# The first unit's rest rows kept in DRAM and multiplied in the last unit, paired with that unit's own

## The chip, the cores and the metric

One core of one Trainium2 chip runs the whole kernel. The metric is the device time of one execution in microseconds; a kernel's time is the median of its runs. In what follows PE is the engine of the matmuls (PEld its weight loads), DVE, ACT and POOL are the vector, scalar and GpSimd engines, and SP is the engine from whose queue nearly all DMAs are issued.

## What is computed

Attention with normalized queries and keys, then a feed-forward block with a squared ReLU:

```
q, k, v: (8, 12, 448, 64)                       # batch, heads, rows, head size
q_n = q / rms(q) * g_q;  k_n = k / rms(k) * g_k
attn = softmax(q_n @ k_n.T / 8) @ v             # for each batch and head
x    = attn put as (8 * 448, 768)               # batch and row, heads side by side
out  = relu(x @ w_in)**2 @ w_out                # w_in (768, 2048), w_out (2048, 768)
```

The weights arrive as 64-bit floats. The kernel loads their words and makes float32 of them itself.

## The kernel before

**Units.** The feed-forward block is done in four units of two batches each (u = 0 to 3, `ffn`). A unit goes through four blocks of the hidden dimension. Each block has a first part (x @ w_in, giving the `hid` tiles) and a second part (hid @ w_out, added into the `acc` tiles). Unit 0's first part is `first_products`: 14 products of COST_IN = 18 in the planner's currency. Later units use `deep_products`. The second part is `second_products`: seven products replace eight (Strassen's scheme in Winograd's form), P1 to P7, over a pair of row tiles, one of each batch of the unit. Each product is two matmuls in the source and four matmul instructions in the trace, because a float32 matmul is issued as two. A product has a cost of COST_OUT = 10.

**Rests.** A batch has 448 rows: three tiles of 128 (NT = 3) and a rest of 64. The two rests of a unit make one tile of 128 rows. Seven products need two such tiles, so a unit's own rests alone can't use them. In units 0 and 3, `multiply_rest` (L1187) multiplies them in the plain way: eight matmuls, 16 instructions, in each block. The rests of units 1 and 2 (`KEPT`) are stored to DRAM block by block (`keep_rests`, L1198), brought back in unit 3 (`bring_rests`, L1214), and multiplied there as one extra pair of tiles by P1 to P7 (tile number NT; its sums are made on POOL by `add_rests`, L1225).

**What a product waits for.** P1 uses a part of `hid` as it stands. P5, P6 and P3 use sums that POOL makes of the four quarters of `hid` (`hidden_sum`, L1173); P7 uses a quarter that POOL changes in place. P5, P6, P7 and P4 also use sums of the output weights (T1 to T4, made at L1539). Three PSUM banks take turns (`roles`); a product may reuse a bank when DVE (L1370) or ACT has taken its contents to an `acc`. In unit 3 the first tile of a block has the order FIRST_OF_BLOCK, in which the two halves of the rests stand where POOL's sums are awaited. In unit 0 the rests come first, before the first P1.

**What is woven into unit 0.** While unit 0 runs, 24 *visits* of attention work for unit 1's batches are put between its products: each gives PE some 8 to 20 instructions (attend L545, score L455) and ACT the exponentials (L463). `run(place(u, x))` lets the products go on until the cost spent reaches a point, then the visit is emitted. Half a visit earlier, tasks are queued that turn the next keys and queries (L367 on DVE, scaled by L377 on ACT). Also in unit 0, the weights of the next blocks are converted in 64 pieces. The call for a piece (`convert`) splits its words on ACT (L1430, L1431, L1433) and joins those of the piece before on DVE (L1444, then L1463 one step later, which gives the buffer back); there are three word buffers, loaded by L1411 (w_in) and L1416 (w_out). The list `late` says at which cost each call is due: before, one every 31.4, evenly. The sums of a finished weight tile are made one at each later step (L1539), and the forms of w_out and of w_in are stored to DRAM for the later units (L1569, L1489, L1517). At the start of block 3's second part the first pieces for unit 1 are loaded back (L902).

**Order.** An engine executes its instructions in the order in which they were emitted. ACT in particular has the copies out of PSUM (L1017), the split of words, the scaling of queries and the exponentials in one row.

Of the kernel before, what the change touches and what calls it, by code (L numbers as in the profile page):

```python
# [225 lines left out]
def program(ctx, tc, rows, v, g, wide, ones, moe_w_in, moe_w_out, out, shift):  # L226
# [711 lines left out]
    FIRST_OF_BLOCK = ["P1", "rest0", "P5", "P4", "P6", "P2", "rest1", "P3", "P7"]  # L938
# [9 lines left out]
    COST_SECOND = (NT * 7 + 4) * COST_OUT  # L948
    COST = NF // 2 * 7 * COST_IN + NBLK * COST_SECOND
    COST_SHORT = NT * 7 * COST_OUT  # L950
    LATER = NBLK * (7 * 11 * COST_DEEP + COST_SHORT)
    KEPT = range(1, B // 2 - 1)
    assert len(KEPT) == 2
# [11 lines left out]
    def ffn(u):  # L965

        accs = []
        for blk in range(NBLK):
# [8 lines left out]
            if u == B // 2 - 1:  # L977
                bring_rests(blk)
                add_rests()
# [195 lines left out]
    PARTS = [(0, 0), (1, 0), (0, 1), (1, 1)]  # L1175
    PARTS_BY_ROW = [(0, 0), (0, 1), (1, 0), (1, 1)]

    def out_of(u, blk):
        return [u * NF // 2 + 2 * blk + t for t in range(2)]

    def multiply_rest(u, blk, hid, places, some, acc=None, halves=range(2)):

        w_sb = [out_sb[n] for n in out_of(u, blk)]
        for half in halves:
            ps = places[half][:, 0:HALF]
            for a, t in some:
                nc.tensor.matmul(  # L1187
                    ps, lhsT=hid[a].rearrange("p t e s -> p t (e s)")[:, t, ds(NT * P, P)],
                    rhs=w_sb[t][:, 2 * a + half, :],
                    start=(a, t) == PARTS[0], stop=(a, t) == PARTS[-1],  # L1190
                )
            if acc is not None:
                add_to(acc[:, ts(half, HALF)], ps, blk == 0)
# [9 lines left out]
    def bring_rests(blk):  # L1203

        if not extra:
            for name in ("11", "12", "S3", "22", "S1", "S2", "S4"):
                some = att.tile([P, S], F32, name="wT", tag="wT", bufs=8)
                extra[name] = some[:, 0 : 2 * P].rearrange("p (t n) -> p t n", t=2)
            extra["accs"] = [
                room.rearrange("p x g h d -> p (x g h d)")[:, 0:DM] for room in rows.rooms  # L1210
            ]
        for u, names in zip(KEPT, (("11", "12"), ("S3", "22"))):
            for a, name in enumerate(names):
                nc.sync.dma_start(extra[name], kept[u][blk, :, a])  # L1214

    def add_rests():

        a11, a12, a21, a22, s1, s2, s4 = [
            extra[name] for name in ("11", "12", "S3", "22", "S1", "S2", "S4")
# [7 lines left out]
    def second_products(u, blk, hid, sums_, accs):  # L1227

        split, final = u in KEPT, u == B // 2 - 1
        if blk == 0:  # L1230
            accs.extend(new_acc() for _ in range(2 * NT if split else 2 * NT + 1))
# [10 lines left out]
        if u:  # L1242
            turn_roles(1, 2, 0)
        else:
            make_sums(0, 1, 2, 3)
            for some in (PARTS[:3], PARTS[3:]):
                multiply_rest(u, blk, hid, roles, some, accs[-1] if (1, 1) in some else None)
                yield len(some) * COST_OUT
            turn_roles(2, 1, 0)

        def store_rows(tt, e, columns=slice(None)):
            if tt is None or tt == NT:
                n = u if tt is None else KEPT[e]
                parts = [(2 * n, P * NT, REST), (2 * n + 1, 0, REST)]
            else:
                parts = [(2 * u + e, REST * e + P * tt, P)]
            store(accs[-1] if tt is None else accs_of(tt)[e], parts, columns)

        def accs_of(tt):
            return extra["accs"] if tt == NT else accs[2 * tt : 2 * tt + 2]  # L1260

        to_store = deque([] if split else [(None, 0)])
# [3 lines left out]
        def product(tt, name, ps, engine):  # L1266
# [5 lines left out]
            for t in range(2):  # L1272
                nc.tensor.matmul(  # L1273
                    ps, lhsT=extra[left][:, t] if tt == NT else lefts[left][:, t, ts(tt, P)],
# [663 lines left out]
```

## Time and profile before

| what | value |
|---|---|
| median of 3 runs | 1381.96 us (1381.06 to 1382.34) |
| the profiled execution: its time / its span | 1381.76 us / 1379.6 us |
| PE busy | 1358.1 us (98% of the span) |
| DVE, POOL, ACT busy | 807.7, 789.8, 608.0 us |
| unit 0 in the span | 129.1 to 487.0 us |
| unit 3 in the span | 1091.8 to 1374.2 us, then the last stores |
| rests, L1187 | 128 matmul instructions, 64 in each of units 0 and 3 |
| products of the second part, L1273 | 1456 matmul instructions, 112 of them on kept rests |

The page gives busy times, the chain of work that ended last, and groups of instructions by line. A busy time of PE counts each matmul from issue to a modelled end, and matmuls overlap; what a matmul costs on the way is read from the chain, where consecutive ones lie end to end. "Idle before, releaser" says what the engine waited for.

### The profile page before, as it was taken

How to read it: one execution, taken by the hardware profiler on the slowest of the kernel's cores; microseconds unless marked ns; L12 is line 12 of the kernel's file. 1: busy time of each engine (PE TensorE's matmuls, PEld its weight loads, DVE VectorE, ACT ScalarE, POOL GpSimd, SP SyncE). 2: the span in 40 equal slices, each digit the busy share in tenths (PEclk: the TensorE clock that was granted, in tenths of full speed). 3: DMA queues.
4: the chain of work that ended last, by engine and by line, in shares of the span. 5: the costliest groups of instructions: out<-in, count | busy, mean ns of one | idle time of the engine just before them, and what ended most of it. 6: DMA issues, size and time to landing. Idle time of an engine off the chain costs nothing.

```text
span 1379.6 us, 19591 instructions
## 1 busy us (share of the span) xinstructions
PE 1358.1 (98%) x6320; PEld 847.1 (61%) x6320; DVE 807.7 (59%) x1635; ACT 608.0 (44%) x1118; POOL 789.8 (57%) x794
## 2 busy tenths in 40 slices
PE   7999999999999999999999999999999999999998
PEld 3333444444444476676758586766768677868684
DVE  4786554877767765555546755455546642445454
ACT  6885477757757144353434244442524032303030
POOL 5668754655555878576667877566745630303030
PEclk9999999999999999999999999999999999999999
DMA  5566846977859867574748666575627451515133
GB/s 145 145 163 181 210 105 162 261 194 195 262 127 276 260 172 211 144 209 101 235 88 238 181 183 178 153 202 128 191 57 255 139 173 63 175 48 193 38 127 105
DMA packets 396101, 230.22 MB, mean 167 GB/s; under 512 B 273621, under 2 KB 357717, under 8 KB 394965
## 3 DMA queue, kind: packets, MB, share of 16 engines
q1 hardware_dynamic: 395696, 228.81, 58.9%
q8 instruction: 52, 0.85, 0.3%
q14 instruction: 61, 0.49, 0.1%
q10 hardware_dynamic: 292, 0.07, 0.0%
HBM read 171.44 MB, written 57.34 MB: 166 GB/s over the span
## 4 chain that ended last, share of the span: by engine, by line
PE 88%; DVE 3%; DMA 2%; ACT 2%; SPq 2%; POOL 2%; issue 1%; POOLq 0%; DVEq 0%; ACTq 0%
PE bank L1273 31%; PE bank L1064 25%; PE bank L1008 8%; PE bank L455 5%; PE bank L545 5%; PE bank L559 4%; PE bank L444 4%; PE bank L1187 2%; PE bank L594 1%; DMA qk<-in_k_dram 1%; PE bank L620 1%; PE bank L611 1%; PE bank L580 1%; DVE acc L1370 1%; PE bank L410 1%
## 5 line engine op out<-in xcount | busy, mean ns | idle before, releaser
L1064 PE MATMUL bank<-xT,in_sb 128*128 128x224 f32 x1344 | 288.0, 353 | 0.0
L1273 PE MATMUL bank<-out_sb,hid 128*128 128x384 f32 x768 | 273.3, 488 | 2.4 <-POOL out_sb L1539 1.4
L1370 DVE TENSOR_TENSOR acc<-acc,bank 128x384 f32<-128x384 f32 x312 | 166.6, 548 | 163.0 <-PE bank L1273 134.1
L1064 PEld LDWEIGHTS bank<-xT,in_sb 128*128 128x128 f32 x1344 | 253.0, 190 | 10.4 <-ACT wT L463 5.6
L463 ACT ACTIVATE wT<-bank,rr 128x448 f32<-128x448 f32 x288 | 163.4, 630 | 159.1 <-PE bank L444 98.2
L1273 PEld LDWEIGHTS bank<-out_sb,hid 128*128 128x128 f32 x768 | 144.9, 190 | 104.7 <-issue 6.2
L1273 PE MATMUL bank<-out_sb,sums 128*128 128x384 f32 x576 | 207.1, 490 | 1.9 <-DVE acc L1370 1.5
L204 POOL TENSOR_TENSOR rr<-ms,minus_half 128x8 f32<-128x8 f32 (+1 forms) x96 | 146.0, 1521 | 71.5 <-DVE ms L197 69.5
L1273 PEld LDWEIGHTS bank<-out_sb,sums 128*128 128x128 f32 x576 | 107.8, 190 | 86.8 <-DVE acc L1370 5.3
L1049 DVE TENSOR_TENSOR hid<-hid,bank 128x224 f32<-128x224 f32 x312 | 111.4, 384 | 83.1 <-PE bank L1064 78.1
L1008 PE MATMUL bank<-xT,in_sb 128*128 128x448 f32 x336 | 131.9, 546 | 0.1
L482 POOL TENSOR_TENSOR sum<-sum,wT 128x448 f32<-128x448 f32 (+1 forms) x96 | 110.9, 1177 | 8.2 <-ACT wT L463 6.6
L1008 PEld LDWEIGHTS bank<-xT,in_sb 128*128 128x128 f32 x336 | 62.2, 190 | 68.9 <-issue 60.1
L455 PE MATMUL bank<-qT,kT 64*128 64x448 f32 (+1 forms) x492 | 99.8, 572 | 1.8 <-DVE qT L418 1.1
L1117 POOL TENSOR_TENSOR hid<-hid 128x448 f32<-128x448 f32 x24 | 27.2, 1141 | 123.1 <-DVE hid L1049 118.7
L482 POOL TENSOR_TENSOR sum<-wT 128x448 f32<-128x448 f32 x48 | 55.7, 1182 | 69.3 <-ACT wT L463 69.3
L1121 ACT ACTIVATE hid<-hid 128x448 f32<-128x448 f32 x96 | 55.0, 573 | 72.2 <-DVE hid L1049 48.4
L444 PE MATMUL bank<-qT,kT 64*64 64x448 f32 x552 | 75.1, 541 | 0.0
L1064 PE MATMUL bank<-more,in_sb 128*128 128x224 f32 x288 | 74.3, 353 | 0.0
L559 PE MATMUL bank<-wT,vt 64*64 64x448 f32 x576 | 73.4, 545 | 0.0
L1061 ACT COPY hid<-bank 128x448 f32<-128x448 f32 x24 | 12.8, 533 | 136.9 <-PE bank L1064 136.1
L455 PEld LDWEIGHTS bank<-qT,kT 64*128 64x128 f32 (+1 forms) x492 | 34.4, 167 | 60.1 <-issue 37.2
(142 smaller groups left out, 2055.5 us busy)
## 6 DMA issues: line engine op xcount, KB each, us to landing
out_sb<-out_forms SPq DMA_DIRECT2D x80, 384.0 KB, 5.1
in_sb<-in_deep SPq DMA_DIRECT2D x64, 384.0 KB, 4.1
in_sb<-in_deep SPq DMA_DIRECT2D x80, 256.0 KB, 4.5
words<-in_moe_w_in_dram SPq DMA_DIRECT2D x32, 384.0 KB, 3.8
words<-in_moe_w_out_dram SPq DMA_DIRECT2D x32, 384.0 KB, 3.7
out_forms<-out_sb SPq DMA_DIRECT2D x8, 1536.0 KB, 6.9
qk<-in_q_dram SPq DMA_DIRECT2D x96, 96.0 KB, 2.7
qk<-in_k_dram SPq DMA_DIRECT2D x96, 96.0 KB, 2.8
```

The lines of the kernel that those rows point to most:

```text
L204: self.nc.gpsimd.tensor_tensor(out=self.rr[i][:, x, 0 : self.count(i)], in0=ms, in1=self.minus_half.to_broadcast(list(ms.shape)), op=ALU.pow,)
L444: nc.tensor.matmul(sc[ds(half * D, D)], lhsT=turned[i, 1][ds(e * D, D), ds(m * P + half * D, D)], rhs=turned[i, 0][ds(e * D, D), :], start ...
L455: nc.tensor.matmul(sc[some], lhsT=turned[p, 1][r, keys], rhs=turned[p, 0][r, :], start=True, stop=True,)
L463: nc.scalar.activation(new_weights((i, m), e), sc, AF.Exp, scale=rows.rr[i][:, 1, 2 * m + e : 2 * m + e + 1],)
L482: nc.gpsimd.tensor_tensor(out=sums[i, e][some], in0=left[some], in1=weights[key_of(i, m), e][some], op=ALU.add)
L545: nc.tensor.matmul(values_bank(i)[ds(e * D, D), :], lhsT=lasts[i % 2][mine, e, :] if m == NJ else values[i][:, m, e, :], rhs=weights[key_o ...
L559: nc.tensor.matmul(bank[ds(e * D, D), :], lhsT=values[i][keys, n, e, :], rhs=weights[(i, n), e][keys], start=n == 0, stop=n == NJ - 1 and ...
L1008: nc.tensor.matmul(ps, lhsT=w_sb[:, IN.index(left), c, :], rhs=forms[u, c][right], start=first and c == 0, stop=c == NK - 1, skip_group_ch ...
L1049: nc.vector.tensor_tensor(out=quarter(name, n), in0=quarter(base, n), in1=ps, op=ALU.add)
L1064: nc.tensor.matmul(ps, lhsT=left, rhs=right, start=start, stop=stop, skip_group_check=True)
L1273: nc.tensor.matmul(ps, lhsT=extra[left][:, t] if tt == NT else lefts[left][:, t, ts(tt, P)], rhs=w_sb[t][:, OUT.index(right), :], start=fi ...
L1370: nc.vector.tensor_tensor(out=acc, in0=acc, in1=ps, op=ALU.add)
```

## The change

The rests of unit 0 are treated as those of units 1 and 2: stored block by block (`KEPT` is now 0, 1, 2). In unit 3 there are two extra pairs of tiles: pair 0 is units 1 and 2 as before, and pair 1 is unit 0's rests from DRAM together with unit 3's own, taken straight from `hid` (`REST_PAIRS`). `multiply_rest` and FIRST_OF_BLOCK are gone. In unit 3 pair 0 now comes first in each block, in the order P1, P5, P2, P6, P3, P4, P7 (it needs nothing of this block but weights), and pair 1 comes before the last tile. Unit 3's first writes into an `acc` go to ACT in that first tile too.

In unit 0 the planner's lengths change: a block costs 252 + 210 in place of 252 + 250. The visits are placed by part: three in each first part (at 84, 168, 252) and three in each second part (at 70, 140, 210). The pieces of weights are due by part as well: the eight of w_out at every 22.5 from the start of a first part, the eight of w_in at every 27.1 from the start of a second part.

```diff
-    FIRST_OF_BLOCK = ["P1", "rest0", "P5", "P4", "P6", "P2", "rest1", "P3", "P7"]
-    COST_SECOND = (NT * 7 + 4) * COST_OUT
-    COST = NF // 2 * 7 * COST_IN + NBLK * COST_SECOND
-    COST_SHORT = NT * 7 * COST_OUT
+    COST_FIRST, COST_SHORT = 2 * 7 * COST_IN, NT * 7 * COST_OUT
+    COST = NBLK * (COST_FIRST + COST_SHORT)
-    KEPT = range(1, B // 2 - 1)
+    KEPT, REST_PAIRS = range(B // 2 - 1), ((1, 2), (0, 3))
...
-                bring_rests(blk)
-                add_rests()
+                bring_rests(blk, hid)
+                add_rests(0)
...
+        for n, us in enumerate(REST_PAIRS):
+            for u, names in zip(us, (("11", "12"), ("S3", "22"))):
+                for a, name in enumerate(names):
+                    if u in KEPT:
+                        nc.sync.dma_start(extra[n][name], kept[u][blk, :, a])
+                    else:
+                        extra[n][name] = hid[a].rearrange("p t e s -> p t (e s)")[:, :, ds(NT * P, P)]
...
             make_sums(0, 1, 2, 3)
-            for some in (PARTS[:3], PARTS[3:]):
-                multiply_rest(u, blk, hid, roles, some, accs[-1] if (1, 1) in some else None)
-                yield len(some) * COST_OUT
-            turn_roles(2, 1, 0)
+            later.append([5, lambda: keep_rests(u, blk, hid)])
...
-        for tt in () if split else (0, NT, 1, 2) if final else range(NT):
+        for tt in () if split else (NT, 0, 1, NT + 1, 2) if final else range(NT):
...
-            order = LAST_ORDER if ends else SECOND_ORDER if tt or not u else FIRST_OF_BLOCK
+            order = LAST_ORDER if ends else FIRST_ORDER if final and tt == NT else SECOND_ORDER
...
+                product(tt, name, roles[PRODUCTS[name][0]][:, 0:HALF], nc.scalar)
+                if final and (tt, name) == (NT, "P1"):
+                    yield from sums_behind_first()
+                    add_rests(1)
                     continue
...
-    every = block / ahead
+    every = ((COST_SHORT - 2 * COST_OUT) / (ahead // 2 - 1), (COST_FIRST - 4 * COST_IN) / (ahead // 2))
     late = deque(
-        block + 2 + every * (n - 2 * tile_pieces) for n in range(len(all_pieces) - ahead)
+        n // ahead * block + (COST_FIRST, block)[m] + 2 + every[m] * (n % (ahead // 2))
+        for n in range(len(all_pieces) - ahead) for m in [n % ahead * 2 // ahead]
     )
...
         if u == 0:
-            return COST * x / unit
+            offsets = [COST_FIRST * n // 3 for n in (1, 2, 3)]
+            offsets += [COST_FIRST + COST_SHORT * n // 3 for n in (1, 2, 3)]
+            block = COST // NBLK
```

## The prediction

> **What bounds the kernel now.** First the head of the page and the chain of waits: PE is on the chain for 88% of the span, at a granted clock of full speed. So a matmul that goes saves its time, unless something else takes its place.
>
> ```profile
> span 1379.6 us, 19591 instructions
> PE 1358.1 (98%) x6320; PEld 847.1 (61%) x6320; DVE 807.7 (59%) x1635; ACT 608.0 (44%) x1118; POOL 789.8 (57%) x794
> PEclk9999999999999999999999999999999999999999
> PE 88%; DVE 3%; DMA 2%; ACT 2%; SPq 2%; POOL 2%; issue 1%; POOLq 0%; DVEq 0%; ACTq 0%
> ```
>
> Second, the chain in order of time (start, length, what), which shows the price of a matmul instruction: rests in unit 3 take 2.58/8 = 0.3225 us, products 29.67/92 = 0.3225 us, and rests in unit 0 stand in the chain with 5.36 us for 16.
>
> ```profile
> 177.71 5.36 PE bank L1187 x16
> 1122.39 2.58 PE bank L1187 x8
> 1132.71 29.67 PE bank L1273 x92
> ```
>
> Third, the same execution cut into stages (PE, PEld, DVE, ACT, POOL busy, clock, DMA share, GB/s): first and second part of unit 0's block 1, the second part of its block 3, and a second part of unit 3. Unit 0 leaves PE gaps of 0 to 2 us in such a part while DMA, and one of ACT, DVE and POOL, are at 75 to 85%; unit 3 leaves everything but PE half empty.
>
> ```profile
> 220.90:264.70 43.80, 43.80 (x142) 18.93 (x140) 30.01 (x51) 35.70 (x65) 23.47 (x19) 1.00 0.78 216
> 264.70:310.70 46.00, 44.85 (x159) 22.17 (x157) 35.69 (x64) 25.22 (x41) 29.01 (x24) 1.00 0.78 209
> 443.20:487.00 43.80, 41.72 (x142) 20.82 (x140) 31.77 (x60) 9.59 (x18) 36.07 (x36) 1.00 0.86 252
> 1191.00:1233.00 42.00, 42.00 (x133) 25.12 (x132) 20.41 (x37) 4.67 (x9) 11.76 (x13) 1.00 0.12 39
> ```
>
> Fourth, where PE waits inside unit 0 (129 to 495 us): 3.8 us in all, most of it on second-part products whose output weights or sums come late.
>
> ```profile
> PE bank L1273 <- DVE acc L1370: 1.8, 3, 0.9
> PE bank L1273 <- POOL out_sb L1539: 1.4, 2, 0.7
> PE bank L455 <- ACT qT L377: 0.6, 1, 0.6
> 275.80 0.91 PE L1273 MATMUL bank<-out_sb,hid 128*128 128x384 f32 x2 [0.46 <-DVE acc L1370]
> 277.40 0.91 PE L1273 MATMUL bank<-out_sb,hid 128*128 128x384 f32 x2 [0.69 <-POOL out_sb L1539]
> ```
>
> **The change part by part. Matmuls.** Unit 0 loses 16 instructions a block, 64 x 0.3225 = 20.6 us. Unit 3 loses 16 and gains a tile pair of 28 a block: 4 x 12 x 0.3225 = 15.5 us more. Together **-5.2 us**, all on PE. That is certain as far as the instructions go; the rest is what waits do.
>
> **Unit 3: no cover is lost.** The rests stood where POOL makes the sums of `hid`; now pair 0's 28 instructions (9.0 us) stand there, longer than the 8.6 us of the four pairs of sums. `add_rests` runs twice: 16 more POOL operations of 0.727 us, 2.9 us a block, against 30 idle us of POOL in a second part of 42. DVE takes 8 results of pair 1 where it took 2 of the rests: 6 x 0.55 = 3.3 us a block beside 20.4 busy of 42, now about 46. The two more loads a block (128 KB, 2.1 us to landing) wait on SP for pair 1's products of the block before, about 9 us from its end; what is queued behind them, the next pieces of w_in, is issued some 25 us later (1277.8 and 1305.5 us now). Hidden. What I charge is block 0 alone, where ACT now makes the first copies while it still has the last Relu and Square (until 1337.7 us in block 3's like place): P5's copy ends near 1338.2, and P3, which wants that bank, stands at 1337.9. **+0.4** (0 to 1).
>
> **Unit 0: waits that go.** The last w_out piece was joined at product 13 of 14 and its sums fell into the second part. By the new list the calls fall at products 1, 2, 3, 4, 6, 7, 8, 9 (before: 1, 2, 4, 6, 8, 9, 11, 13), so four steps are left for the sums. The 0.46 + 0.69 us above, and the same pair (0.52 + 0.68) in block 3, should go: 2.35 us at most, 0 at least if DVE is late for other reasons. I take **-2.0**.
>
> **Unit 0: a wait that comes.** Four calls in a row put four word splits (2.1 us each) on ACT while PE does 4 x 2.32 us. The fourth piece's buffer is given back only by L1463 of the first, so its load can't be issued earlier than the one which in block 3 now goes at 409.26. Loads land after 3.1/3.7/5.3 us.
>
> ```profile
> 409.26 0.35 SPq L1416 DMA_DIRECT2D words<-in_moe_w_out_dram  x1
> 413.86 0.67 ACT L377 ACTIVATE qT<-qT,g 128x448 f32<-128x448 f32 x1 [1.45 <-DVE qT L367]
> 414.60 0.21 PEld L455 LDWEIGHTS bank<-qT,kT 64*64 64x64 f32 x8 [0.65 <-issue]
> DMA to landing us min/median/max: 3.1/3.7/5.3
> ```
>
> The split then holds ACT from 413.0 to 415.1, and queued behind it is the scaling of queries L377 (0.65 us), for which PE's last scores of this visit wait: they stand at 414.6 and can start at 415.75. That is 1.1 us (0.5 with a landing of 3.1, 2.7 with 5.3). In block 1 the same load goes at 230.75 and gives the same. Blocks 0 and 2 have no such visit there. **+2.2** (1.0 to 5.4). The copies out of PSUM behind a late split are not late for PE: a bank is wanted again two products, 4.6 us, later, and a visit of 3.4 us often lies between.
>
> **The start of a second part without rests.** P5 needs POOL's first sum, and 5.4 us of cover are gone. What covers it now is the visit that already stands at that place (2.5 us in blocks 1 and 3, 4.3 in blocks 0 and 2) and P1 and P2 (2.6 us).
>
> ```profile
> 444.02 1.41 POOL L1173 TENSOR_TENSOR sums<-hid 128x384 f32<-128x384 f32 x1 [3.30 <-ACT hid L1157]
> 459.13 0.65 DVE L367 STREAM_TRANSPOSE kT<-qk 128x448 f32<-128x448 f32 x1 [4.80 <-DMA qk<-in_k_dram]
> ```
>
> In block 3 PE would be at P5 at 443.27 + 2.58 = 445.85 and the sum is done at 445.43; the later ones come 1.0 to 1.1 us apart for products 1.3 us apart. I charge 0 (0 to 2, half a us in each block).
>
> **Block 3's second part** has the DMAs full (the burst of first pieces for unit 1), and DVE waits there 4.8 us for keys. Now that wait lies under slack; with PE 5.2 us ahead it need not. After the visit, seven products (9.0 us), the next visit (3.4) and one P1 (1.3) go on without DVE, from 444.4 to 458.1; the bank wanted next is free at about 460.3 if the keys land as now. That is 2.2 us. Against it: the 1.5 MB store of w_out forms at 440.8, 5 us of transfer at some 300 GB/s, moves ahead by four products. I take **+1.0** (0 to 2.2).
>
> Also moved: unit 0's eight stores of rests, 1 MB against some 72 MB moved in unit 0 (GB/s by length, summed over its parts), and its eight DVE adds less; nothing.
>
> **Sum.** -5.2 + 0.4 - 2.0 + 2.2 + 1.0 = -3.6 us against the profiled execution's 1381.76 us (span 1379.6 and 2.2 around it): 1378.2. The median of the runs shown is 0.2 higher, which changes nothing. With each term at its best: -5.2 - 2.35 + 1.0 = -6.5; at its worst: -5.2 + 1 + 5.4 + 2 + 2.2 = +5.4.
>
> A rule of the Trainium skill speaks against the change. "TensorE: Matmul & The Clock Gate", in "HAM oscillation — how this bites in real kernels", asks for "no PE-idle gaps >~3.4µs", since an idle window halves PE's clock and a busy one must pass before it is back. The rows: the longest wait of PE in unit 0 is 0.9 us and the clock granted is 1.00 in every part of it. By the rows a wait costs its own length; by the page one that outgrew the window would cost about 1.7 us on top, an estimate (its window of some 3.4 us run at half clock), and the sum would be 1379.9 with one such wait.
>
> **Rivals.** *The clean case:* ACT's slack is larger than I hold it to be, because the fourth load lands on DMAs that are a third busy (0.32 between 405 and 410 us), and the earlier stores relieve block 3. Then only the 5.2 and 2.35 remain: 1374.3. Against it: the margins above are below 1.2 us. *The slow case:* the three word buffers. A buffer is held from the issue of its load until the second call after its split, so in a dense row of calls a load's landing time stands in ACT's way, in front of the query scaling on which PE waits. Each us of landing costs two (blocks 1 and 3). With the sum at -3.6 at 3.7 us, it decides from a landing of 5.5 us on; at 7.8 us, the longest that the w_in words show, it is +4.6: 1386.4. For it: ACT waited for words 13 times, 30.2 us in all, even with even spacing, and the DMA share is 0.95 to 1.05 in half of these stages. Against it: the first four loads fall where DMAs are still idle. *The last block bound by DMA:* if block 3's second part can't get shorter than its transfers let it (0.86 of 43.8 us = 37.7 us of DMA time, 38.6 us left for PE), its 5.2 us are lost: 1383.4 with the rest of the sum, 1382.4 without the 1.0 already charged there. For it: the share is above 1.0 from 442 to 462. Against it: it falls to 0.2 to 0.7 from 474 to 498, so transfers can move back. *That the matmuls do not go* is no rival: the count is in the loops.
>
> **How the numbers follow.** A measurement of this kernel tells a time from no change at about 0.2%, 2.8 us: faster is below 1379.2, slower above 1384.7. My sum 0.41 (its own range 1375 to 1382: 0.28 faster, 0.11 within, 0.02 slower); clean case 0.27, faster; slow case 0.21, slower; last block 0.11 (0.01, 0.09, 0.01). So faster 0.56, within 0.20, slower 0.24. The range goes from 1373.5, a little under the clean case, to 1385.0, which leaves out the far half of the slow case.
>
> **What would show it.** In unit 0, L1187 gone and the second parts 4 to 6 us shorter; in unit 3, four stretches of L1273 that are 3.9 us longer and no wait in them. The waits on L1539 gone. A wait of PE's L455 on L377 of about 1 us in blocks 1 and 3 right after product 5: much longer, and the slow case holds. L367 in block 3 tells the last. The prediction is wrong if unit 0 is not at least 15.5 us shorter, or if PE waits at the start of second parts on L1173.

## The result, and the profile after

The changed kernel takes 1385.1 us (median of 9 runs, 1383.87 to 1390.75) beside 1381.96 us for the kernel before (9 runs, 1381.06 to 1383.94). The ratio is 1.0028, 95% interval 1.0019 to 1.0036: it is slower by about 0.3%, where 1378.2 was forecast. The profiled execution took 1384.19 us.

In this profile L1006 are the products of the first part (L1008 before), L1260 those of the second part (L1273), L1346 and L1342 their adds by DVE and ACT (L1370, L1366), L1406 to L1409 the split of words (L1430 to L1433), L1392 the load of w_out words (L1416), L1475 the derived forms of w_in (L1499), L1515 the sums of weights (L1539). First the head of its page and its chain of waits:

```profile
span 1382.4 us, 19667 instructions
PE 1358.1 (98%) x6304; PEld 844.4 (61%) x6304; DVE 817.9 (59%) x1647; ACT 608.7 (44%) x1122; POOL 804.1 (58%) x810
PE 82%; DVE 5%; DMA 5%; ACT 3%; SPq 3%; issue 2%; POOL 1%; ACTq 0%; POOLq 0%; DVEq 0%
```

Sixteen matmul instructions went, as the diff says (6320 to 6304). PE's part of the chain fell from 88% to 82%: DVE, DMA, ACT and SP's queue took it over. Cut by the first matmul of each part, the span goes as follows (us; "forecast" is the sum of the prediction's terms for that stage):

| stage | before | after | difference | forecast |
|---|---|---|---|---|
| up to unit 0 | 129.1 | 129.6 | +0.4 | 0 |
| unit 0, four first parts | 181.6 | 186.6 | +5.0 | +2.2 |
| unit 0, four second parts | 182.0 | 163.3 | -18.7 | -21.6 |
| units 1 and 2 | 598.9 | 599.1 | +0.2 | 0 |
| unit 3 and the end | 288.0 | 303.8 | +15.9 | +15.9 |
| span | 1379.6 | 1382.4 | +2.8 | -3.5 |

By this cut unit 0 of the kernel before ends at 492.7 us, with its last visit of attention; 487.0, given further above, is where its last products end. Unit 3 came out as forecast. Unit 0 lost 7 of the 20.6 us that its matmuls should have given. The same execution by stages (PE, PEld, DVE, ACT, POOL busy, clock, DMA share, GB/s): first and second part of block 1, second part of block 3, and a second part of unit 3. The last row is the whole second part of block 3 in the kernel before:

```profile
216.40:262.25 45.85, 44.85 (x142) 19.10 (x140) 31.53 (x52) 35.09 (x64) 26.35 (x22) 1.00 0.82 229
262.25:303.45 41.20, 40.32 (x142) 19.10 (x140) 32.04 (x60) 25.11 (x42) 26.70 (x23) 1.00 0.78 208
433.85:479.45 45.60, 43.03 (x182) 20.63 (x180) 33.89 (x61) 12.56 (x23) 37.83 (x37) 1.00 0.80 227
1184.10:1228.00 43.90, 43.90 (x138) 25.88 (x137) 22.24 (x40) 2.77 (x5) 13.54 (x16) 1.00 0.09 27
443.27:492.74 49.47, 47.39 (x199) 23.54 (x197) 35.48 (x66) 12.69 (x24) 41.73 (x41) 1.00 0.81 235
```

The first part of block 1 was 43.80 us with PE never idle; it is now 45.85 with a full us of idling, for the same products. (The other us counts as busy, since the records of the scores run on into their wait.) The second parts of blocks 0 and 2 have their 5 us less. That of block 1 has 4.7, and not the further us that PE's waits for late sums and for DVE had cost; that of block 3 has 3.9. No engine but PE is full in any of these stages, and unit 3's is PE alone. So the loss is in single waits. Those of PE in unit 0 (129 to 482 us), by what they waited for:

```profile
PE bank L1260 <- DVE acc L1346: 2.6, 4, 1.4
PE bank L611 <- ACT wT L463: 2.3, 2, 1.7
PE bank L455 <- ACT qT L377: 1.8, 4, 0.8
```

Before, the list had POOL's weight sums (1.4), DVE (1.8) and L377 (0.6). The weight sums are gone from it, DVE's part has grown, L377's has tripled (0.84 of it lies in block 3's second part, where the queries come late from DVE, and no words are in it), and L611, the row sums of the softmax, is new. The instructions themselves, on ACT, then PE's weight loads for the scores in blocks 1 and 3, then PE (start, length, what, and in brackets the idling before it and its cause):

```profile
230.35 0.57 ACT L1406 ACTIVATE words<-words 128x384 f32<-128x384 f32 x1 [2.70 <-DMA words<-in_moe_w_out_dram]
232.21 0.62 ACT L377 ACTIVATE qT<-qT,g 128x448 f32<-128x448 f32 x1
328.60 0.56 ACT L1406 ACTIVATE words<-words 128x384 f32<-128x384 f32 x1 [4.46 <-DMA words<-in_moe_w_out_dram]
337.62 2.19 ACT L463 ACTIVATE wT<-bank,rr 128x448 f32<-128x448 f32 x4
...
232.88 0.20 PEld L455 LDWEIGHTS bank<-qT,kT 64*64 64x64 f32 x4 [1.12 <-ACT qT L377]
405.23 0.19 PEld L455 LDWEIGHTS bank<-qT,kT 64*64 64x64 f32 x4 [1.01 <-ACT qT L377]
...
232.89 0.97 PE L455 MATMUL bank<-qT,kT 64*64 64x448 f32 x4 [0.34 <-ACT qT L377]
254.04 0.97 PE L611 MATMUL bank<-sum,ones 128*64 128x448 f32 x4 [0.65 <-ACT wT L463]
339.96 0.97 PE L611 MATMUL bank<-sum,ones 128*64 128x448 f32 x4 [1.69 <-ACT wT L463]
```

ACT stands 2.70 us at the fourth piece's words, then splits them in 2.1 us, and only then scales the queries: PE's scores wait. That was forecast, at 1.1 us in each of blocks 1 and 3. The whole visit, from its first matmul to the next product, takes 4.81 us in block 1 (228.97 to 233.78) where it took 3.52 (233.47 to 236.99), so 1.3 us more; in block 3 it is 1.2 more. What was not forecast: in block 2 ACT stands 4.46 us at words until 328.60, and what it has to do then leaves no room for the delay: this split, two more, and Relu, Square and copies between them run with almost no gap until 337.6. The exponentials L463 come only then, nine us after the words. L611 writes into a PSUM bank that these exponentials must empty first; PE stands 1.69 us there. In block 1 it is 0.65. The words of block 2 were late for a reason that SP's queue shows:

```profile
315.99 3.94 SPq L1465 DMA_DIRECT2D in_deep<-in_sb  x3
319.97 2.70 SPq L1467 DMA_DIRECT2D in_deep<-in_sb  x2
322.78 1.28 SPq L1392 DMA_DIRECT2D words<-in_moe_w_out_dram  x1
```

The five raw stores of w_in take SP 6.6 us to issue, the load of words stands behind them, and its transfer then meets theirs (the DMA share is 1.15 and then 1.07 from its issue to the split): 5.8 us from its issue to the split. In block 1 a load behind the same stores takes 7.1 us (issued at 235.92, split from 243.00).

In the second parts DVE is late (DVE and PE):

```profile
263.24 2.43 DVE L1475 TENSOR_TENSOR more<-in_sb 128x384 f32<-128x384 f32 x2 [1.09 <-DMA in_deep<-more]
448.89 0.65 DVE L367 STREAM_TRANSPOSE kT<-qk 128x448 f32<-128x448 f32 x1 [5.69 <-DMA qk<-in_k_dram]
...
268.07 1.56 PE L1260 MATMUL bank<-out_sb,hid 128*128 128x384 f32 x4 [0.33 <-DVE acc L1346]
270.18 1.56 PE L1260 MATMUL bank<-out_sb,sums 128*128 128x384 f32 x4 [0.55 <-DVE acc L1346]
450.03 1.56 PE L1260 MATMUL bank<-out_sb,hid 128*128 128x384 f32 x4 [1.38 <-DVE acc L1346]
```

In block 1 DVE waits until a derived form of w_in has been stored and its buffer is free, works off its row, and PE misses two banks (0.33 and 0.55 us) where before it missed one bank (0.46) and one weight sum (0.69). In block 3 DVE waits 5.69 us for keys, and PE 1.38 behind it.

### The profile page after: what moved, and what is told of

It reads as the page before. It is cut to its first block, busy times and chain, and to the rows that moved or that the text cites. A ratio compares the mean times of both kernels' runs of the same rounds, so it can differ in the third digit from the quotient of the medians.

```text
span 1382.4 us, 19667 instructions
## 1 busy us (share of the span) xinstructions
PE 1358.1 (98%) x6304; PEld 844.4 (61%) x6304; DVE 817.9 (59%) x1647; ACT 608.7 (44%) x1122; POOL 804.1 (58%) x810
## 4 chain that ended last, share of the span: by engine, by line
PE 82%; DVE 5%; DMA 5%; ACT 3%; SPq 3%; issue 2%; POOL 1%; ACTq 0%; POOLq 0%; DVEq 0%
PE bank L1260 33%; PE bank L1062 25%; PE bank L455 4%; PE bank L559 4%; PE bank L444 4%; PE bank L545 4%; PE bank L1006 3%; DMA words<-in_moe_w_out_dram 2%; DMA qk<-in_k_dram 1%; PE bank L594 1%; DVE more L1475 1%; PE bank L620 1%; SPq L318 1%; DVE acc L1346 1%; PE bank L580 1%
## 5 line engine op out<-in xcount | busy, mean ns | idle before, releaser
L1260 PE MATMUL bank<-out_sb,hid 128*128 128x384 f32 x800 | 285.6, 489 | 2.1 <-DVE acc L1346 2.1
L1346 DVE TENSOR_TENSOR acc<-acc,bank 128x384 f32<-128x384 f32 x300 | 160.0, 548 | 146.3 <-PE bank L1260 136.9
L463 ACT ACTIVATE wT<-bank,rr 128x448 f32<-128x448 f32 x288 | 163.9, 631 | 135.1 <-PE bank L444 95.9
L1260 PEld LDWEIGHTS bank<-out_sb,hid 128*128 128x128 f32 x800 | 149.8, 190 | 114.3 <-issue 9.5
L1260 PE MATMUL bank<-out_sb,sums 128*128 128x384 f32 x576 | 205.8, 489 | 1.7 <-DVE acc L1346 1.2
L1260 PEld LDWEIGHTS bank<-out_sb,sums 128*128 128x128 f32 x576 | 108.1, 190 | 83.9 <-DVE acc L1346 4.8
L1006 PE MATMUL bank<-xT,in_sb 128*128 128x448 f32 x336 | 131.9, 546 | 0.3 <-DVE hid L1148 0.3
L1115 POOL TENSOR_TENSOR hid<-hid 128x448 f32<-128x448 f32 x24 | 27.3, 1142 | 176.4 <-DVE hid L1047 172.0
L455 PE MATMUL bank<-qT,kT 64*128 64x448 f32 (+1 forms) x492 | 104.4, 573 | 3.0 <-ACT qT L377 1.8
L1006 PEld LDWEIGHTS bank<-xT,in_sb 128*128 128x128 f32 x336 | 62.1, 190 | 69.3 <-issue 60.2
L1119 ACT ACTIVATE hid<-hid 128x448 f32<-128x448 f32 x96 | 55.0, 573 | 72.9 <-DVE hid L1047 48.4
L455 PEld LDWEIGHTS bank<-qT,kT 64*128 64x128 f32 (+1 forms) x492 | 35.6, 167 | 64.7 <-issue 36.2
```

The costliest lines, as they stand in the source:

```text
L455: nc.tensor.matmul(sc[some], lhsT=turned[p, 1][r, keys], rhs=turned[p, 0][r, :], start=True, stop=True,)
L463: nc.scalar.activation(new_weights((i, m), e), sc, AF.Exp, scale=rows.rr[i][:, 1, 2 * m + e : 2 * m + e + 1],)
L1006: nc.tensor.matmul(ps, lhsT=w_sb[:, IN.index(left), c, :], rhs=forms[u, c][right], start=first and c == 0, stop=c == NK - 1, skip_group_ch ...
L1260: nc.tensor.matmul(ps, lhsT=lefts[left][:, t, ts(tt, P)] if tt < NT else extra[tt - NT][left][:, t], rhs=w_sb[t][:, OUT.index(right), :], ...
L1346: nc.vector.tensor_tensor(out=acc, in0=acc, in1=ps, op=ALU.add)
```

## The experiments

Each was timed beside the kernel before; ratios are to that kernel. "The changed kernel" is the starting point unless the kernel before is named.

### What the rests were worth in unit 0

The kernel before, with unit 0's rests left out: they are neither multiplied, added nor stored (the seventh `acc` tile of unit 0 goes with them), and their cost still passes in the planner, so no other call moves.

```diff
             for some in (PARTS[:3], PARTS[3:]):
-                multiply_rest(u, blk, hid, roles, some, accs[-1] if (1, 1) in some else None)
                 yield len(some) * COST_OUT
...
```

> The kernel before, with unit 0's rests left out (not multiplied, added or stored; their 40 of cost a block still pass, without work). Theory words (ACT stands still for words of weights because of the new dense list of calls; the list of before is even): nothing dense here, so unit 0 gives the full 64 x 0.3225 = 20.6 us and the time is about 1361 to 1363. Theory cover (the rests hid work of DVE and POOL at the start of second parts): 2 us or more are lost in unit 0's second parts, 1364 or more.

Measured: 1384.57 us, ratio 1.0026 (1.0016 to 1.0036). It does 64 matmul instructions less and takes longer: the theory of cover holds, at a price of 22.8 us (20.6 and 2.2) where it named 2 or more. The four second parts of unit 0 take 184.2 us in place of 182.0. Its waits of PE in unit 0, and then two stretches by stages:

```profile
PE bank L1272 <- POOL out_sb L1538: 9.7, 3, 3.9
PE bank L1272 <- DVE acc L1369: 4.9, 4, 2.0
...
```

```profile
365.30:368.00 2.70, 2.62 (x6) 1.03 (x8) 0.56 (x1) 0.87 (x1) 2.20 (x3) 0.50 0.89 208
456.40:459.00 2.60, 2.53 (x6) 0.95 (x8) 1.34 (x3) 0.00 (x0) 2.60 (x5) 0.50 0.86 236
```

The rests stood where the last sums of w_out were awaited. Without them PE waits 9.7 us for these sums (L1538 here), in three waits of 2.7, 3.1 and 3.9 us, and behind each of them the granted clock is 0.50 to 0.57. So the rests of unit 0 cost next to nothing on the path: they were cover. To have the 20.6 us, these sums have to come earlier. That is what the change's denser list of conversions does, and everything that the list brings with it is part of the price.

### The visits where they were before

```diff
         if u == 0:
-            offsets = [COST_FIRST * n // 3 for n in (1, 2, 3)]
-            offsets += [COST_FIRST + COST_SHORT * n // 3 for n in (1, 2, 3)]
-            block = COST // NBLK
+            return COST * x / unit
```

> The changed kernel with the visits of unit 0 spread evenly over the cost as before, the list of calls for words left as changed. Theory places (visits collide with late work at the new places): back by 3 us or more, 1382 or less. Theory words: the calls are as dense as in the changed kernel, 1384 to 1387, ACT's waits for words near 34 us in unit 0 as now.

Measured: 1399.14 us, 1.0123 (1.0107 to 1.0138). Its waits of PE in unit 0:

```profile
PE bank L611 <- ACT wT L463: 7.2, 3, 3.9
...
PE bank L1260 <- POOL sums L1171: 2.4, 4, 0.6
```

Neither theory had this; by the one of places it should have been faster. The exponentials behind the words cost three times as much; and in all four blocks PE now waits for POOL's first sum of `hid`, because no visit stands at the start of a second part. The placing of the visits is thus worth 14 us with this list of calls, and it is what covers that start.

### Fewer words at a time, two weight sums a step

```diff
-    every = ((COST_SHORT - 2 * COST_OUT) / (ahead // 2 - 1), (COST_FIRST - 4 * COST_IN) / (ahead // 2))
+    every = ((COST_SHORT - 2 * COST_OUT) / (ahead // 2 - 1), 27.9)
...
             make_sum()
+            if first and sums_to_make:
+                make_sum()
```

> The changed kernel with the w_out calls at every 27.9 in place of 22.5 (after products 1, 2, 4, 5, 7, 8, 10, 11), which leaves two steps for the sums of the last tile, so two sums are made at each step. Theory words: ACT waits for words 10 us less in unit 0, PE's first parts are 2 to 3 us shorter in all, 1382 to 1383. Theory cover: first parts gain nothing that the later sums don't take back, 1385 or more.

Measured: 1399.92 us, 1.0142 (1.0126 to 1.0157), a miss. SP's queue, ACT and PE in block 1:

```profile
230.00 1.46 SPq L1392 DMA_DIRECT2D words<-in_moe_w_out_dram  x1
...
236.66 0.54 ACT L1406 ACTIVATE words<-words 128x384 f32<-128x384 f32 x1 [7.97 <-DMA words<-in_moe_w_out_dram]
...
239.14 1.76 PE L455 MATMUL bank<-qT,kT 64*64 64x448 f32 x4 [7.27 <-ACT qT L377]
```

The second sum a step lets the raw stores of w_in come earlier, and on SP's queue they now stand, from 224.54, ahead of an earlier load of words than before: 5.4 us for issuing them, and then 6.7 us from the load's issue at 230.00 to its split (in the changed kernel the load of the fourth words goes at 226.70, ahead of them, and ACT splits at 230.35). ACT stands 8.0 us, and PE 7.3, in blocks 1 and 3 alike: 14.6 us in two waits. This is the slow case of the prediction in pure form: a late landing of words is a late scaling of queries. But the run does not tell what less density alone would do, since it moved the stores as well. It led to the run in which the stores alone are moved, further below.

### A fourth buffer for words

```diff
-        return ffn_p.tile([P, HALF, 2], U32, name="words", tag="words", bufs=3)
+        return ffn_p.tile([P, HALF, 2], U32, name="words", tag="words", bufs=4)
...
-        to_load.append([2, n + 2])
+        to_load.append([2, n + 3])
...
     load_weights(1)
+    load_weights(2)
...
-        return ffn_p.tile([P, DM], F32, name="acc", tag="acc", bufs=2 * NT + 1)
+        return ffn_p.tile([P, DM], F32, name="acc", tag="acc", bufs=2 * NT)
```

The room comes from the seventh `acc` tile, which the change no longer needs.

> The changed kernel with four word buffers and loads one piece earlier; the room comes from the acc tiles, six in place of seven. Theory words: a load has one call more to land, so ACT's waits for words in unit 0 fall from 34 us to under 10, the first parts of blocks 1 to 3 lose 4 of the 5 us that they lost, and the time is 1380 to 1382, if the attention before unit 0 doesn't suffer from six acc tiles. Theory cover or places: 1384 to 1386, with ACT's waits gone and PE's time the same.

Measured: 1378.65 us (11 runs), 0.9979 (0.9970 to 0.9988): faster than both kernels. Its waits of PE in unit 0, the first and second part of block 1 by stages, and ACT at the place shown above:

```profile
PE bank L1260 <- DVE acc L1346: 1.1, 2, 0.7
PE bank L455 <- ACT qT L377: 0.8, 1, 0.8
```

```profile
215.72:260.20 44.48, 44.48 (x142) 19.08 (x140) 32.89 (x52) 35.71 (x65) 25.51 (x22) 1.00 0.82 236
260.20:300.20 40.00, 40.00 (x142) 19.27 (x140) 30.70 (x60) 24.47 (x41) 26.70 (x22) 1.00 0.80 214
```

```profile
226.89 0.57 ACT L1406 ACTIVATE words<-words 128x384 f32<-128x384 f32 x1
230.84 0.67 ACT L377 ACTIVATE qT<-qT,g 128x448 f32<-128x448 f32 x1 [1.82 <-DVE qT L367]
```

The fourth split starts at 226.89 without a wait, and the scaling now waits for nothing but its own transposition. ACT's waits for words in unit 0 fall from 22.3 + 12.2 us (w_out, w_in) to 0.2 + 3.9, the waits at L611 are gone, and PE is never idle in block 1. By the first matmuls of its parts, unit 0 is 343.7 us long, 19.9 less than before: nearly all of the 20.6. Its first parts take 182.2 us (186.6 in the changed kernel, 181.6 before), its second parts 161.5 (163.3 and 182.0). The control is the next run.

### The control: six `acc` tiles and nothing else

```diff
-        return ffn_p.tile([P, DM], F32, name="acc", tag="acc", bufs=2 * NT + 1)
+        return ffn_p.tile([P, DM], F32, name="acc", tag="acc", bufs=2 * NT)
```

> The changed kernel with six acc tiles in place of seven and nothing else: the other half of the run with four word buffers. If the fourth word buffer alone made that run 6 us faster than the changed kernel, this one is within 1 us of the changed kernel, 1384 to 1386; if the acc tiles had a part in it, 1382 or less.

Measured: 1385.89 us, 1.0026 (1.0015 to 1.0036), as the changed kernel. The gain is of the word buffers with their earlier loads.

### A fifth buffer for derived forms

```diff
-        ... tag="more", bufs=4)
+        ... tag="more", bufs=5)
```

Also with six `acc` tiles.

> The changed kernel with a fifth buffer for the derived forms of w_in (the room again from six acc tiles), three word buffers. Theory cover (at the start of the second parts of blocks 1 and 3 DVE waits until a derived form is stored, which the rests used to hide): DVE's wait there goes, PE's waits for acc in blocks 1 and 3 fall by 1 to 2 us, 1383 to 1384. Theory words alone: first parts as slow as before, 1384 to 1386, no gain.

Measured: 1384.33 us (11 runs), 1.0019 (1.0010 to 1.0028). DVE's waits for a free buffer of these forms, first in the changed kernel, then in this one:

```profile
DVE more L1475 <- DMA in_deep<-more: 8.6, 4, 6.6
```

```profile
DVE more L1475 <- DMA in_deep<-more: 1.2, 3, 0.6
```

With them PE's two waits behind DVE in block 1 go (0.33 and 0.55), and its second part takes 39.8 us in place of 41.2: 6.1 less than before the change, the 5.2 of the matmuls and nearly 1 of the late sums. The waits in block 3 stay (0.35 and 1.38 in the changed kernel, 0.50 and 0.87 here). So the buffer is what made DVE late in block 1. In the time it is 0.8 us, or 1.6 beside the control with six `acc` tiles, and the intervals overlap. With four word buffers the same waits of PE in block 1 are gone too, though DVE still waits 9.2 us for these buffers: its first add stands 2.3 us behind the first matmul of that part, where it is 3.3 in the changed kernel and 1.9 here. Why words in time bring DVE forward was not traced.

### Block 3: the first loads for unit 1 spread out

```diff
                     for n in range(4):
-                        load_piece(n, False)
-                        load_piece(n, True)
+                        for m in (False, True):
+                            later.append([3 + 3 * n, partial(load_piece, n, m)])
```

> The changed kernel with the nine first loads for unit 1, issued at once at the start of block 3's second part, spread over twelve products. Theory burst: the keys behind them land 3 us sooner, PE's wait of 1.4 us for an acc in block 3 goes and with it about 1.5 us: 1383 to 1384. Theory words: 1384 to 1386, first parts unchanged.

Measured: 1387.91 us, 1.0044 (1.0030 to 1.0059). Block 3's second part is 42.2 us in place of 45.6 and its 1.38 us wait is gone, but PE in unit 1 then stands here:

```profile
514.96 2.58 PE L1062 MATMUL bank<-xT,in_sb 128*128 128x224 f32 x6 [2.79 <-DMA in_sb<-in_deep]
```

The 3.4 us gained are spent on pieces that now come late, and some more: unit 1's first two blocks take 84.1 us where they took 76.7, and behind the wait shown the granted clock is 0.50 from 514.9 to 521.0. The transfers must be done at about this time; what can be chosen is who waits for them.

### Without the stores of unit 0's rests

Unit 0's rests aren't stored, and unit 3 loads those of unit 1 in their place.

```diff
-                        nc.sync.dma_start(extra[n][name], kept[u][blk, :, a])
+                        nc.sync.dma_start(extra[n][name], kept[max(u, 1)][blk, :, a])
...
-            later.append([5, lambda: keep_rests(u, blk, hid)])
```

> The changed kernel without the stores of unit 0's rests; unit 3 loads those of unit 1 a second time in their place, so the rows of unit 0's rests are not the reference's. Theory words, cover and burst alike: eight stores of 128 KB are nothing beside the rest of unit 0's transfers, 1384 to 1386. A theory that the stores themselves delay unit 0's loads: 1383 or less.

Measured: 1387.91 us (5 runs, 1385.36 to 1389.87), 1.0043 (1.0028 to 1.0057). Unit 1 starts at 480.5 us beside 479.5. The stores are not what unit 0 loses by. The profiled execution is slower by 1.2 us in unit 0 (a wait of 1.02 us of L455 behind L377 in block 1's second part), by 0.9 in unit 1's first two blocks and by 0.8 behind the start of unit 3's last block; why was not found.

### The scaling of queries on DVE

```diff
-            nc.scalar.mul(dst, dst, g)
+            nc.vector.tensor_scalar(out=dst, in0=dst, scalar1=g, scalar2=None, op0=ALU.mult)
```

> The changed kernel with the scaling of the queries (L377) moved from ACT to DVE, right behind the transposition that it reads; nothing else differs. In the changed kernel the products of the scores (L455) of unit 0's blocks 1 and 3 start 1.3 and 1.2 us late by my reading, because the scaling stands on ACT behind a words split that waits for its load; the products of the row sums (L611) lose another 2.4 us behind exponentials (L463), which stay on ACT. Theory (ACT's wait for words is the cause, by way of what stands behind it on ACT): the waits at L455 behind L377 go and those at L611 stay: some 2.5 us less than the changed kernel, 1382.5 us, still near or above the kernel before. Rival (the first parts are late by their DMAs or their transpositions, and ACT's order is no cause): the waits at L455 stay in size and are put down to another releaser: 1385 us. Second rival: DVE's sums then come later, and as much is lost at the second products (L1260 behind DVE acc): 1385 us with the wait moved.

Measured: 1383.41 us (11 runs), 1.0018 (1.0009 to 1.0027). Its waits of PE in unit 0, and the longest of them behind DVE:

```profile
PE bank L1260 <- DVE acc L1346: 4.5, 5, 2.2
PE bank L611 <- ACT wT L463: 2.5, 2, 1.4
...
```

```profile
449.92 2.93 PE L1260 MATMUL bank<-out_sb,hid 128*128 128x384 f32 x4 [2.16 <-DVE acc L1346]
```

All waits at L455 are gone, and still the first parts of blocks 1, 2 and 3 are only 0.15, 0.14 and 0.5 us shorter than in the changed kernel (block 0's is 1.4 shorter, where no word was late: the scores of its last visit, which had stood behind Relu and Square on ACT, take 1.94 us in place of 3.02, and a wait of 0.31 is gone). In block 1 the visit with the scores is 0.6 us shorter, and 0.4 of it turned up at the next thing that ACT owes, L611 (1.09 in place of 0.65). And block 3's second part is 2.3 us longer, behind a fuller DVE; 1.6 of it is the half clock of the last section. Moving one of the late operations off ACT moves the wait; what makes ACT late has to go. Both the theory and its second rival held in part.

### The raw stores behind the loads of words

```diff
-            for n, some in enumerate((upper[:, :, 0], upper[:, :, 1], lower[:, :, 1])):
-                nc.sync.dma_start(keep[:, :, PLACES[n]], some)
...
+            for m, (n, some) in enumerate(parts):
+                send = partial(nc.sync.dma_start, keep[:, :, PLACES[n]], some)
+                if first:
+                    later.append([m + 1, send])
```

One of the five is issued at each of five steps, behind the load of words that falls into that step.

> The changed kernel with the five raw stores of w_in (L1465, L1467) issued one at each of five steps, each behind that step's load of words, instead of all five at once ahead of it; three word buffers as in the changed kernel. In the changed kernel these five stand on SP's queue from 315.99 to 322.67 in block 2, a load of words follows at 322.78, ACT waits 4.46 us for it, and L611 waits 1.69 us behind the exponentials; in block 1 they stand from 229.75 to 235.81, and L611 waits 0.65. Theory (SP's order is the cause of the late words there): the load goes some 6 us earlier, ACT's wait of 4.46 and both waits at L611 go, while those at L455 (0.34 in block 1, whose load goes at 226.70 ahead of the stores) stay: 2.3 to 2.7 us less than the changed kernel, 1382.5 us. Rival (the buffers are the cause: the load's buffer isn't free before that time anyway): the load goes no earlier, 1385 us. A third way: the stores then delay the loads after them, and the wait moves to another piece: 1384 to 1387 us.

Measured: 1386.84 us (5 runs), 1.0035 (1.0021 to 1.0049). Its waits of PE in unit 0:

```profile
PE bank L1260 <- DVE acc L1346: 5.4, 5, 1.9
PE bank L455 <- ACT qT L377: 1.5, 3, 0.8
PE bank L611 <- ACT wT L463: 0.5, 1, 0.5
```

The theory holds for the first parts: the load of block 2 goes at 318.21 instead of 322.78, ACT's waits for w_out words fall from 22.3 to 12.5 us, block 2's wait at L611 is gone, and its first part is 45.1 us instead of 46.9. The one in block 1 stays against the theory (0.53 where it was 0.65): there ACT now waits 2.84 us for words of w_in ahead of the exponentials. Those at L455 stay, with their own cause, the buffer. But the second parts lose more than that: 42.6 in place of 41.2 us in block 1, and 48.8 in place of 45.6 in block 3, behind DVE and with a stretch of 3.4 us at a granted clock of 0.51. It is the third way of the expectation: the raw stores now lie among the loads of w_in words and the stores of derived forms, and these come late. ACT's waits for w_in words are 25.8 us in place of 12.2, and DVE's for a buffer of derived forms 15.2 in place of 8.6.

### Four word buffers, and DVE for unit 3's first tile

```diff
-                product(tt, name, roles[PRODUCTS[name][0]][:, 0:HALF], nc.scalar)
+                product(tt, name, roles[PRODUCTS[name][0]][:, 0:HALF], nc.vector if tt == NT else nc.scalar)
```

> The changed kernel with four word buffers (the version that took 1378.65 us) and, besides, the two tiles of rests' first tile in unit 3 adding its first block's products by DVE instead of ACT. In the changed kernel PE stood about 0.3 to 0.4 us in unit 3's first block behind ACT's copies of P1, P5 and P6 out of the banks. Theory: that gap closes and nothing else moves: 0.3 us less than with four buffers alone, some 1378.3 us, which may not be told from no change. Rival: DVE is behind there with the sums of the hidden values and loses more than ACT did: 1379 to 1380 us.

Measured: 1379.11 us (12 runs), 0.9988 (0.9980 to 0.9997). The chain in unit 3's block 0 with four word buffers alone (its pieces between these lines run through DVE L1115, ACT L1119 and the copy L1342), and then with DVE as well:

```profile
1102.67 0.77 PE bank L1062 x4
...
1106.85 0.47 ACT qk L1342
...
1107.36 40.26 PE bank L1260 x124
```

```profile
1102.13 0.76 PE bank L1062 x4
1102.89 43.86 PE bank L1260 x136
```

The detour by ACT's copy is gone, and from unit 3's first piece of the chain to the last one on PE it is 297.86 us in place of 298.20: 0.34 less, the +0.4 of the prediction. The times don't show so little. That a second version with four word buffers is faster than the kernel before confirms the first.

### The same, with the raw stores spread

The edits of the last two experiments together.

> The version with four word buffers and DVE for unit 3's first tile (1379.11 us), with the five raw stores of w_in spread over five steps behind the loads of words. Theory: with four buffers no load of words is late for ACT any more (3.9 us of waiting in all of unit 0), so the order on SP's queue has nothing left to give: 1379 us, within a us. Rival (the stores still hold up something else on SP's queue, such as keys and queries): some us less, 1376 to 1378.

Measured: 1382.0 us (11 runs), 1.0000 (0.9991 to 1.0009). It is not 1379, as the theory had it, and still less the gain of the rival: PE waits 2.90 us behind DVE in block 1's second part, and DVE has just waited 3.69 us for a buffer of derived forms. The words had nothing left to gain, and the stores had something to lose: their old place, all at once, was the better one for what stands behind them.

## Why the prediction was wrong

- **Matmuls, -5.2:** right. They went from unit 0 and came to unit 3 as counted.
- **Unit 3, block 0, +0.4:** right (0.34 by the run with DVE in its first tile), and the rest of unit 3 had no wait.
- **"A wait that comes", +2.2:** right in mechanism and in size. The scores of blocks 1 and 3 wait behind L377 and the late words (PE's weight loads 1.12 and 1.01 us), the two visits are 1.3 and 1.2 us longer, and the load that was estimated to land after 3.7 us landed within 3.7 (issued at 226.70, split from 230.35).
- **What failed first: "The copies out of PSUM behind a late split are not late for PE".** It is true of the copies here (with the visits spread and with two sums a step, PE does wait 1.18 and 3.71 us behind them), but the exponentials L463 stand in the same row of ACT, and a PSUM bank waits for them. The prediction had no term for L611; it looked for the scaling of queries alone, and so let block 2 off ("Blocks 0 and 2 have no such visit there"), where the largest of these waits fell. They are 2.3 us listed: 1.69 in block 2, which came of SP's order (with the raw stores moved it is gone), and 0.65 in block 1, which stays when the stores move and is gone with the fourth word buffer. With them the first parts lost 5.0 us (2.5 + 2.3 and 0.2 in block 0), not 2.2.
- **What failed second: "Waits that go", -2.0.** The weight sums are no longer late, but PE gets nothing for it. Of the 2.35 us that the prediction put down to them, 0.98 (the 0.46 and 0.52) were waits for DVE by the rows. In block 1 DVE, held by a buffer of derived forms, is late for two banks in their place (the fifth buffer showed this): the second part there gave 4.7 us, not 6.2. The prediction had given 0 only "if DVE is late for other reasons", and took nearly the maximum.
- **Block 3, +1.0:** right in mechanism, with keys awaited for 5.69 us and 1.38 us of PE behind it; the 0.84 at L455, which is late queries, had no term. The second part gave 3.9 of its 5.2 us, so 1.3 were lost net, and the -1.0 that it should have had from its sums did not show. The row that the prediction takes for this part stops at 487.00, ahead of the last visit. The whole part is 49.47 us with 0.81 of DMA share, so 40.1 us of DMA time stood against 44.3 left for PE, not 37.7 against 38.6: the rival of a last block bound by DMA was weaker than it looked there.
- **"The start of a second part without rests", 0:** right. No wait on the sums of `hid` in the changed kernel, and 2.4 us of them when the visits are moved away from that place.

Against the forecast the first parts miss 2.8 us, nearly all of it the first failed step, and the second parts 2.9: 1.5 in block 1, the second failed step, 1.3 in block 3 and 0.2 in block 2. Together they are nearly all of the 6.0 between 1378.2 and the profiled 1384.19. Of the rivals the slow case came nearest, 1386.4, and its mechanism, words that come late to ACT because there are three buffers, is the one that the fourth buffer shows. That its number came near is in part luck. Its price was laid to a landing of 7.8 us in front of the scores of blocks 1 and 3, and there the landing was the usual one; what came were landings of 5.8 us in block 2 and 7.1 in block 1, behind stores on the same queue and in front of the exponentials, and a loss of like size in the second parts. A fourth buffer mends both causes, since every load is then issued one piece earlier.

The 0.4 us before unit 0 say nothing: in the profiled executions of the other versions unit 0 starts anywhere from 128.6 to 130.0 us. What stays open: why the run without stores of rests is slower, why the second part of block 1 is also mended by words in time, and whether block 3's loss can be had back at all, since every run that relieved it by more than 1 us lost as much elsewhere.

## What to carry to other kernels

Before counting the matmuls that a change removes, ask what they covered: here 20.6 us of them could be left out with no gain at all, because weight sums were late behind them. A change that brings late work forward needs its buffers deeper in the same step; one more word buffer, in room that the change itself had freed, turned +0.3% into -0.2%, while taking out one wait singly (the scaling on DVE, the stores spread, the loads spread) gave it back, in whole or for the most part, at another operation. And when an engine is late, list everything that stands behind it in its row, and price each for its own reader, not the first one alone.

## What the runs showed of the hardware

How long PE waits once does not tell here whether its clock falls. In the scaling-on-DVE run a wait of 2.16 us was followed by a stretch at half clock (columns as above):

```profile
449.90:453.00 3.10, 3.08 (x5) 1.85 (x6) 3.10 (x6) 0.00 (x0) 2.53 (x3) 0.50 1.05 381
```

Four matmuls there took 2.93 us in place of 1.56 and the eight after them 3.08 in place of 2.85, so the wait cost 1.6 us more than its length. The run with the visits where they were before has both sides: the clock stayed at 1.00 behind a listed wait of 2.86 us (253.47, PE busy for 0.61 of the 3.47 us before it) and fell to half behind one of 1.23 (449.85, PE busy for 2.03 of the 3.85 before it):

```profile
253.47:257.00 3.53, 3.53 (x11) 1.63 (x12) 3.16 (x6) 2.16 (x5) 3.53 (x4) 1.00 1.03 363
450.60:454.00 3.40, 3.40 (x7) 1.89 (x6) 3.37 (x4) 0.00 (x0) 3.24 (x4) 0.50 0.99 301
```

It also fell behind 1.86 us with the raw stores spread (438.32), and stayed behind 2.90 in the last run (267.80). The Trainium skill ("TensorE: Matmul & The Clock Gate", "HAM oscillation — how this bites in real kernels") puts the limit at gaps of about 3.4 us: the price that the prediction worked out from it, about 1.7 us, agrees with the scaling-on-DVE run; the limit does not decide it here, as single listed waits of 1.23 to 2.16 us were enough. What else decides was not found.

SP needs 0.35 us to issue a load of words in most places, but 6.6 us for the five raw stores of w_in forms in block 2 of the changed kernel. The load that stands behind them takes 3.6 us to land in the median, so an issue can cost more time on its queue than the transfer that waits behind it.
